# The parts of the maxima's rows on GpSimd instead of VectorE, with a changed pace of block A, sums one step later and a new hand-written order, in a kernel of two attention blocks

## The chip, the cores and the metric

The kernel runs on one core of one Trainium2 chip. The metric is the device time of one execution in microseconds (us). The time before is the median of three runs.

## The reference, cut to what matters

Two independent attention blocks over 2048 positions of width 640, 32 heads of 20, are computed and their outputs stand side by side. Block A looks at 8 positions (its own and every second one before it), block B at all 2048.

```python
def _A_ref(x, wqkv, wo):            # block A: a window of 8, dilation 2
    ...
    logits = jnp.einsum("bhsd,bhswd->bhsw", q, kg) * scale
    logits = jnp.where(mask[None, None, :, :], logits, -1e9)
    attn = _softmax(logits, axis=-1)
    o = jnp.einsum("bhsw,bhswd->bhsd", attn, vg)
    return (lambda x, *d: x.transpose(*d))(o, 0, 2, 1, 3).reshape(B, S, D) @ wo

def _B_ref(x, wqkv, wo):            # block B: full attention
    ...
    scores = jnp.einsum("bhqd,bhkd->bhqk", q, k) * (Dh ** -0.5)
    p = _softmax(scores, axis=-1)
    o = jnp.einsum("bhqk,bhkd->bhqd", p, v)
    return (lambda x, *d: x.transpose(*d))(o, 0, 2, 1, 3).reshape(B, S, D) @ wo

return jnp.concatenate([a, b], axis=-1)
```

## The kernel before, in words

**Stages.** First come the projections of A and of B and the rows of v of B. Then one long loop of 488 steps does nearly all of B's attention and, beside it, most of A's. Behind the loop stand 24 steps of B without maxima, and the output projection of B.

**Block B in the loop.** B is cut into 32 units (8 groups of 4 heads by 4 chunks of 512 queries), and a unit into 16 steps of 128 keys. One step needs, for each of the four heads, the following.

- A score matmul with keys on the partitions (`s_matmul`; output 128 x 512), and on ScalarE the exponential of it out of PSUM (`s_exp`, tile `e`).
- The matmuls of that `e` with v (`b_pv`, four accumulations side by side). After every second step ScalarE copies the sum to SBUF: the first of a unit to the tile `braw`, the seven others to a tile `more`, which GpSimd adds to `braw` (`pool(raws[u], raws[u], more)`). There are four `more` buffers, so that one comes round every eight steps.
- The maxima that a softmax needs. They are computed a second time from scores with queries on the partitions (`m_matmul`), 24 steps ahead (`LEAD`), and reduced out of PSUM by VectorE (tile `mx`).

When the maxima of a unit are complete, `max_rows` brings them into the two extra rows of the query tile `bq`, by which the score matmul subtracts them: VectorE reduces 64 values a partition to 16 and transposes 128 x 32 (`raw`), then splits that into a rounded part and the rest of it (tile `mtr`: one copy and one subtraction of 128 x 32). SP stores the parts to DRAM (`mdr`, four transfers), and loads them as rows of `bq` (two transfers). The steps of this are put off with `after(n, ...)`, which calls a function n steps later when the instructions are written out. A step is a place in the program, not a time.

**Order of the loop.** All engines run their instructions in the order in which the program writes them. A string `ORDER` writes the loop's order out by hand. `S` is two score halves, `Y` a score half and a maximum half, `M` and `N` two maximum halves with one reduction of 1024 columns or two of 512, `V` a step's `b_pv` (it also calls `begin`, which counts the step), `F` a piece of A's output projection and `j` a transpose of A. Digits name the PSUM banks. Eight banks serve all of it.

**Block A in the loop.** A goes in 16 tiles of 128 rows, each with eight units: four make scores (tile `akv` times `aq`, then halving sums into `al`), four weigh the values (`akv` times `al`, then sums into `ao`). All of that is GpSimd's. Between the two lies a softmax, of which VectorE does the maximum (`am`) and the reciprocal as "soft jobs". VectorE transposes the result (`turn`), DMAs carry it out and back, GpSimd splits it (`aot`) and `F` multiplies it with the output weights. Sixteen of the 128 units are done ahead of the loop.

**A's pace.** The class `InOrder` adds up an estimate of GpSimd's time, `gp.us`: for each tensor operation a constant and an amount per element. In each step from `A_FROM` on, `begin` writes out further instructions of A while the estimate is below step number x `STEP` (2.47 us) + `AHEAD` (2.4 us). All of GpSimd's tensor operations count in it, the sums of `braw` too.

**Names.** The profile gives every instruction one line, L66, the helper that writes them out; so its tiles tell them apart. Buffer numbers are left out (`mx4`, `mx1` are `mx`).

Of the kernel before, what the change touches and what calls it, by code (L numbers as in the profile page):

```python
# [10 lines left out]
F32 = mybir.dt.float32  # L11
# [37 lines left out]
A_FROM = 4  # L49


class InOrder:
# [6 lines left out]
    def __getattr__(self, name):  # L59
        op = getattr(self.engine, name)  # L60

        def emit(*a, **k):
            if name.startswith("tensor_"):
                n = math.prod(a[0].shape[1:])
                self.us += 0.25 + n * (0.00081 if name == "tensor_copy" else 0.00212)
            return self.tc.keep_in_program_order(op(*a, **k))  # L66
        return emit
# [3 lines left out]
def attention_pair(ctx, tc, xa, wqk_a, wv_a, wo_a, xb, wqk_b, wv_b, wo_b, oa, ob):  # L71
# [295 lines left out]
    def a_softmax(t):  # L367
# [8 lines left out]
        job(soft_jobs, 0, lambda: dve.tensor_reduce(m[:, 0], L.rearrange("p o h -> p h o"), AX.X, ALU.max))  # L376
# [11 lines left out]
        job(soft_jobs, 0, lambda: dve.reciprocal(m[:, 0], m[:, 0]))  # L388
# [217 lines left out]
    def max_rows(m4, m1, q, qc):  # L606
# [22 lines left out]
        after(t + 1, store)  # L629
        after(t + 2, load)  # L630
# [95 lines left out]
    def b_pv(i):  # L726
# [187 lines left out]
    def begin(i):  # L914
# [25 lines left out]
        "Y07M1S36M4V0Y71M4M2S06V7Y06M2S14Y75V0Y16M2S74VY71M5S42S03N17V4Y05S61M2VY07M5S13S42N70V1S36M4S72VY03M4S76V2Y30"  # L940
        "S17M4VjY03S16M4Y72V3S01jM4Y67VY02M4S61S73jY02jV6M4S71Y23VS70M4jS13Y26V7M4S01Y63VN05S41S23Y67M4S01N27V3S04M5Y21"
        "VY07M5S42S13N07V4S56M1Y03VY75S06M1Y34V7Y06S51M2VY06M4S13Y72V6Y03M4S17VY03M1S74Y56V3Y70M1S45VjY07S64Y51M2S07jV6"
        "jM4S13Y02VM4S73S02Y16jM4Y73jS06V2Y71M4S03VY07S16M4S32N70V1Y36M4S72VY07M2S64S51N70V6Y52M3S71VY70M1Y53S46V7M4S02"
        "Y61VN02S35M6S41S03N52V4Y07M5S31VY70M2S16S45N07V1Y26M3S05VY07M5Y24S31Y70V2Y13M5S74VY70M3S15Y26V7M0Y53S24VM0S26"
        "M4F3Y07M1S64Y35V0Y74S16M2VY71M4S63Y02V7S61M4Y03VY62S01M4Y37V6Y02S51M3VY70M1S53Y46V0Y75S13N24VN71S26M3S50S72N16"
        "V5Y70M3S21VY07M1S63S45N70V6Y14M2S75VY70M4S13jS26jV7jM0N53S42VN04S12Y56F7jjY05M1S36Y74V0Y35M1S76VY73M4S62Y01V7"
        "Y62M4S03VY06M1S35Y47V6Y03S52N14VN70S15M2N46F7Y05S41M2Y76V0S15M2Y74VS15M6Y23N04F1Y07S62M3Y51V0Y72S36M4VY71M2S64"
        "Y05Y17V6Y02M3S51VY70M1S53S46N07V5Y41M2S06VY70Y61M2S45Y07V6Y51S24Y03VM1S73Y45V0Y17M2S65VS71M5S42N30V7S61M4Y32V"
        "S06Y15N43N27F0Y16S52M3Y70V1Y26M3S75VY07M5S24S31N70V2S36M4Y71VY03S74M5Y12V0M3S75Y16VM3S75Y21V6S70N34Y51VY70M3"
        "S52Y16V7Y05S42N31VS06jS52jY34N17jF0jjY71S26M4Y03V7S62M4S01VM2S04Y56V1S07M2Y46VY07S25M3Y61V7Y02M3S56VY05M1S63"  # L950
        "S47N05V6S41M2Y70VY15S74M2Y06V1S75M2Y04VY75S06M2Y14V7Y06S53M1VY06M4S31S72N60V3Y74S56M1VY07M4S61S32N70V6Y51M3S72"
        "VY70M1S53S46N07V5Y41M2S06VY70Y61S42Y35S07N61V4Y35N62S01VM5Y70N13S24F7Y06M4Y12S73V0Y17M4S63VY71M2S64Y05V7Y64M2"
        "S01VY06M4Y13S72Y60V1Y72M4S36VY07M2S64S51N70V6Y52S73N41VY70S52M3Y16V7Y05M3S21VY02M5S14Y73V0Y14S25M6VjS14jM2M6"
        "Y50F1jjjY72M3S05Y61V7S02M3S65VM0S26Y34V5Y70M1S64VY07S63M1Y45V7Y60M1S34VS06M3S52N17V0S63Y45M1VY73M5S42S01N73V4"
        "Y05M6S12VY05M1S37S64N50V3Y27S16M4VY70M1S64S35N07V6Y41M2S05VY70M4S13S26N07V1Y25M3S06VY07M5S24S31N70V2S36M4Y71V"
        "Y03S74M5Y12F0Y71M5S42Y03V7Y42M5S01VY04M2S15Y76V0Y15M2S74VY71M5S42S30N17V4Y35S62M0VY73M5S20S14N37V2Y01M5S34VY70"
        "M3S15S26N07V1S25M3Y06VY72S03M4Y61V7S02jM4Y63VS02jS16jM4N37F0jjY71S26M4Y03V7Y62M4S01VY06M2S14Y75V0Y16M2S74VS71"
        "M5S42N30V7S61Y54M2VS04M5S17M2S04Y56V1Y07M2S46VY07S45M2S61N70V4Y35M6S21VY05M1S37S64N50V3Y27S16M4VY70M1S64S35N07"
        "V6Y41M2S05VY70M4S13S26N07V1Y25M3S06VY07M5S24Y31V0Y72M5S43VS71M3S25N60V7S14N32S65VM3Y06N21F5Y07M3S26Y51V0Y72S36"
        "M4VY71M2S64Y05V7Y64M2S01VY06M4S13Y27V6Y01M4S32VN70S13S24Y56N71V0Y26M3S75VY71M5S24Y03V1Y27M5S40VjY72M3M5S01jF7j"  # L960
        "jjY06S51M3Y72V0Y16M3S75VY71M5S24S03N17V2Y06S15M3VY07M5S14Y32V7Y01M5S43VS04M1S35N67V0S14Y32M5VS74M2S10M5S74Y32"
        "V1Y07M5S24VY07S23M5S41N70V2Y36M4S71VY07S16M4S32N70V1Y36M4S72VY07M2S64S51N70V6Y52M3S71VY70M1S53S46N07V5S41M2Y06"
        "VY74M2Y01S65V7Y06S24N35VY06M3M1S57F0Y73S46M1Y05V7S64M1S03VM5S04Y12V3Y07M5S42VY70S14M5Y23V0Y17M5S42VY71M3S25Y60"
        "V1Y72M3S56VY07M5S24S31N70V2Y36M4S71VY07Y16M4S32Y70V1S26M4Y73VY02M4M6S31jF0jjjY71M4S63Y02V7Y61M4S03VY06M1S35Y74"
        "V0Y35M1jS76VY73M4S62Y10V7Y62M4S31VS06M2S14Y57V0Y16M2S47VY14M5S72S30N41V7Y62M3S05VY06M1S53S74N06V5S73M1Y04VY73"
        "S06M1M4S73V0Y17M2S64S51M6VY52M3S17S06N25V1Y07M3S26VY07M5S24Y31V0Y72M5S43VS71M3S25N60V7Y14M2S65VY04S15M6S23N04"
        "V1S27N65Y03VY72S06M4N13F7Y02S14M5Y73V0Y14S25M6VY14M2S57S06N41V5Y07M2S46VS70Y16M2Y45V7Y60M2S14VY06M4S13Y72V6Y01"
        "M4S37VjS03jM1M4Y76F0jjjY71S26M4Y03V7Y62M4S01VY06M2S14S75N60V1Y72S36M4VY07M2S64S51N70V6Y52M3S71VY70M1S53S46N07"
        "V5S41M2S06VY74S03M1V6Y75S40M1VY75M3S02Y16V5Y70M3S21VY07M1S63S45N70V6Y14M2S75VY70M4S13S26N07V1Y25M3S06VY07M5S24"
        "S31N70V2Y36M4S71VY07Y16M4S32S70Y16V3Y27M4S06VN70S12M4S63Y71V0Y26S53N47VY16S25M3S70N61V2Y73S46N05VS71Y06M3N52F7"  # L970
        "Y06S15M3Y72V0M5S14Y73VM1S46Y75V3Y40S21M5VY70S42M5Y13V0Y74M5S21VjS74jM1M5Y30F7jjjY61M2S04Y75V6Y04M2S71VY70M4S13"
        "S26N07V1Y25M3S06VY07M5S24S31N70V2Y36M4S71VY07Y16M4S32Y70V1Y26S53N74VS02S73M5V4Y02S17M5VY03S12M5Y74V3Y01S25N67V"
# [12 lines left out]
        "Y03V7Y62M4S01VY06M2S14S75N60V1Y72S36M4VY07M2S64S51N70V6M2S75Y41VY70S52M3V1M6S05Y43VS07M5Y42V3Y70S16M4VY70S61j"
        "S25jM3N07F6jjjY70M3S52Y16V7Y05M3S21VY02M5S14Y73V0Y14M5S72VY71M3S25S06N17V2Y03S14M5VY70M3S15S26N07V1Y25M3S06V"
# [11 lines left out]
    for kind, *ns in re.findall("[A-Zj][0-7]*", ORDER):  # L998
# [90 lines left out]
```

## Time and profile before

| | us |
|---|---|
| median of three runs (1826.25 to 1831.67) | 1831.59 |
| the profiled execution's own time | 1828.4 |
| its span, first to last instruction | 1826.4 |
| busy in the span: TensorE, VectorE, ScalarE, GpSimd | 1779.4, 1387.3, 1328.9, 1197.8 |

In the profile PE is TensorE, PEld its weight loads, DVE VectorE, ACT ScalarE, POOL GpSimd and SP the queue that issues the DMAs. A group's row gives its count (x), its busy time, the mean of one in ns, and the engine's idle time just ahead of it with what ended that. The row of a window gives its length, and then busy time and count of each engine in the order PE, PEld, DVE, ACT, POOL, followed by the granted TensorE clock (1.00 is full), the DMA engines' share and GB/s; asked for one tile, it shows only the engines that work on that tile. A row of a timeline is start, duration, engine, operation, and in brackets the idle time ahead of it. The three score matmul groups of B are `ps_st<-bq,bk` (maxima), `ps_st<-bk,bq` (scores) and `ps_st<-e,vb` (values).

### The profile page before, as it was taken

Reading aid. Unit: us, or ns where it says so; the run is one execution under the profiler, and the core shown is the slowest. Engines: PE = TensorE matmul, PEld = TensorE weight load, DVE = VectorE, ACT = ScalarE, POOL = GpSimd, SP = SyncE. Lnnn points to the kernel's source line nnn. Section 1 sums busy time; section 2 is a strip of 40 time slices with the busy share of each in tenths; the row PEclk is TensorE's granted clock in tenths of the full one; section 3 lists DMA queues with packets and bytes.
Section 4 is the critical chain, followed back from the end, with each engine's and each line's share of the span. In section 5 each row is a group of like instructions: output and inputs, shape, how many; then the busy total and the mean of one; then the engine's idle time right before and its main releaser. Section 6 shows DMA issues by size and latency. Waiting matters only on the chain.

```text
span 1826.4 us, 31534 instructions
## 1 busy us (share of the span) xinstructions
PE 1779.4 (97%) x11211; PEld 997.6 (55%) x11211; DVE 1387.3 (76%) x1872; ACT 1328.9 (73%) x2593; POOL 1197.8 (66%) x1008
## 2 busy tenths in 40 slices
PE   9999999999999999999999999999999999999999
PEld 8988888887434444444444444444443443444469
DVE  3000333278999999999999999999999999999400
ACT  4222322223998899999899898989888888989981
POOL 0000079027899788898899898888888887635442
PEclk9999999999999999999999999999999999999999
DMA  6333687754642544353354425433533442212123
GB/s 229 114 97 114 199 300 259 245 171 135 178 131 82 135 131 124 112 163 112 114 138 114 138 89 160 139 116 90 162 116 104 120 129 92 48 51 80 50 69 111
DMA packets 191189, 240.21 MB, mean 132 GB/s; under 512 B 89020, under 2 KB 115260, under 8 KB 190040
## 3 DMA queue, kind: packets, MB, share of 16 engines
q1 hardware_dynamic: 190456, 237.54, 43.4%
q8 instruction: 88, 1.44, 0.3%
q14 instruction: 69, 0.57, 0.1%
q10 hardware_dynamic: 576, 0.66, 0.1%
HBM read 173.21 MB, written 64.91 MB: 130 GB/s over the span
## 4 chain that ended last, share of the span: by engine, by line
PE 69%; DVE 23%; DMA 2%; POOL 2%; issue 2%; ACT 2%; SPq 0%; DVEq 0%; POOLq 0%; ACTq 0%
PE ps_st L66 69%; DVE mx L66 20%; DVE mtr L66 3%; DMA bk<-kb_d 2%; ACT e L66 1%; POOL akv L66 1%; POOL braw L66 0%; DMA s_d<-braw 0%; DMA akv<-va_d 0%; DVE turn L66 0%; DMA akv<-ka_d 0%; DVE am L66 0%; ACT more L66 0%; POOL aot L66 0%; DMA bq<-qb_d 0%
## 5 line engine op out<-in xcount | busy, mean ns | idle before, releaser
L66 DVE TENSOR_REDUCE mx<-ps_st 128x1 f32<-128x512 f32 (+1 forms) x1486 | 1214.5, 884 | 50.1 <-PE ps_st L66 47.1
L66 ACT ACTIVATE e<-ps_st 128x512 f32<-128x512 f32 x2048 | 1065.4, 614 | 68.8 <-PE ps_st L66 49.4
L66 PE MATMUL ps_st<-bq,bk 62*128 62x512 f32 x2048 | 559.6, 441 | 23.1 <-DVE mx L66 21.7
L66 PE MATMUL ps_st<-bk,bq 60*128 60x512 f32 x2048 | 543.6, 444 | 16.5 <-DVE mx L66 14.4
L66 PE MATMUL ps_st<-e,vb 128*32 128x512 f32 x4096 | 548.1, 610 | 1.2 <-ACT e L66 0.3
L66 PEld LDWEIGHTS ps_st<-bq,bk 62*128 62x128 f32 x2048 | 279.5, 185 | 467.2 <-ACT e L66 280.4
L66 POOL TENSOR_TENSOR braw<-braw,more 128x512 f32<-128x512 f32 x224 | 288.3, 1287 | 191.0 <-ACT more L66 187.9
L66 POOL TENSOR_TENSOR akv<-akv,aq 128x1280 f32<-128x1280 f32 x64 | 188.5, 2945 | 234.6 <-DMA akv<-ka_d 234.6
L66 PEld LDWEIGHTS ps_st<-bk,bq 60*128 60x128 f32 x2048 | 248.5, 185 | 117.4 <-DVE mx L66 70.6
L66 POOL TENSOR_TENSOR akv<-akv 128x640 f32<-128x640 f32 (+3 forms) x304 | 283.7, 933 | 14.2
L66 ACT COPY ro<-ps_st 128x320 f32<-128x320 f32 (+2 forms) x124 | 61.4, 497 | 221.9 <-PE ps_st L66 172.5
L66 PEld LDWEIGHTS ps_st<-e,vb 128*32 128x32 f32 x4096 | 82.2, 108 | 154.9 <-issue 75.0
L66 POOL TENSOR_TENSOR akv<-akv,al 128x1280 f32<-128x1280 f32 x64 | 152.1, 2376 | 0.2
L66 ACT COPY more<-ps_st 128x512 f32<-128x512 f32 x224 | 133.8, 597 | 11.8 <-PE ps_st L66 9.3
L66 PE MATMUL ps_st<-wc,xn 128*128 128x512 f32 (+1 forms) x576 | 133.4, 376 | 0.0
L66 PE MATMUL ps_st<-ww,xn 128*128 128x320 f32 x768 | 127.6, 317 | 0.0
L66 PEld LDWEIGHTS ps_st<-ww,xn 128*128 128x128 f32 x768 | 114.9, 190 | 20.1 <-ACT e L66 7.9
L66 PEld LDWEIGHTS ps_st<-wc,xn 128*128 128x128 f32 x576 | 106.4, 188 | 17.6 <-ACT xn L66 0.2
L66 PE MATMUL ps_st<-xn,w 128*128 128x512 f32 x480 | 115.8, 390 | 0.0
L66 PEld LDWEIGHTS ps_st<-xn,w 128*128 128x128 f32 x480 | 90.1, 188 | 19.4
L66 ACT CAST pr<-ps_st 128x512 fp32r<-128x512 f32 x40 | 23.6, 589 | 101.0 <-PE ps_st L66 101.0
L66 DVE TENSOR_TENSOR pr<-ps_st,pr 128x512 fp32r<-128x512 f32 x40 | 27.7, 692 | 90.6 <-ACT pr L66 87.8
(64 smaller groups left out, 1027.3 us busy)
## 6 DMA issues: line engine op xcount, KB each, us to landing
akv<-ka_d SPq DMA_DIRECT2D x128, 320.0 KB
akv<-va_d SPq DMA_DIRECT2D x128, 320.0 KB
kb_d<-pr SPq DMA_DIRECT2D x20, 512.0 KB
qb_d<-pr SPq DMA_DIRECT2D x20, 512.0 KB
bk<-kb_d SPq DMA_DIRECT2D x16, 640.0 KB
bq<-qb_d SPq DMA_DIRECT2D x64, 160.0 KB
rb<-s_d SPq DMA_DIRECT2D x128, 64.0 KB
stg<-xb SPq DMA_DIRECT2D x12, 512.0 KB
```

Of the source, the lines that this page charges most:

```text
L66: return self.tc.keep_in_program_order(op(*a, **k))
```

## The change

1. The copy and the subtraction behind the transpose of a unit's maxima move from VectorE to GpSimd (`parts`). The store of them is written out one step later, and the load too.
2. A soft job of A's softmax may be written out by `begin` three steps after it is given; before, it was written out at the start of A's next unit.
3. The estimate of GpSimd's time has a constant of 0.2 us instead of 0.25, and 0.0017 us instead of 0.00212 an element for the operations with four dimensions (the weighing of the values). A starts at step 1 instead of 4.
4. The sum of `braw` and `more` is written out two steps after the copy instead of one.
5. A piece of A's output that isn't ready at its `F` is kept (`owed`) and tried again at each later step; before, its bank stayed in the list of given banks.
6. `ORDER` is new. In both strings a unit's maxima are complete 7 to 10 steps ahead of its first score matmul, and there are 488 `V` and 32 `F`.

| in `ORDER` | S | Y | M | N | reductions (M + Y + 2N) | steps from one pair of F to the next | step of the last F |
|---|---|---|---|---|---|---|---|
| before | 661 | 630 | 514 | 147 | 1438 | 30.9 on average | 466 |
| after | 647 | 658 | 517 | 130 | 1435 | 28.5 on average | 434 |

```diff
-A_FROM = 4
+A_FROM = 1
...
-                self.us += 0.25 + n * (0.00081 if name == "tensor_copy" else 0.00212)
+                self.us += 0.2 + n * (0.00081 if name == "tensor_copy" else 0.0017 if len(a[0].shape) == 4 else 0.00212)
...
-        job(soft_jobs, 0, lambda: dve.tensor_reduce(m[:, 0], L.rearrange("p o h -> p h o"), AX.X, ALU.max))
+        job(soft_jobs, 3, lambda: dve.tensor_reduce(m[:, 0], L.rearrange("p o h -> p h o"), AX.X, ALU.max))
...
-        job(soft_jobs, 0, lambda: dve.reciprocal(m[:, 0], m[:, 0]))
+        job(soft_jobs, 3, lambda: dve.reciprocal(m[:, 0], m[:, 0]))
...
             dve.transpose(raw, m1)
-            dve.tensor_copy(mt[:, 1], raw)
-            dve.tensor_tensor(mt[:, 2], raw, mt[:, 1].bitcast(F32), ALU.subtract)
+
+        def parts():
+            gp.tensor_copy(mt[:, 1], raw)
+            gp.tensor_tensor(mt[:, 2], raw, mt[:, 1].bitcast(F32), ALU.subtract)
...
         after(t, turn)
-        after(t + 1, store)
-        after(t + 2, load)
+        after(t, parts)
+        after(t + 2, store)
+        after(t + 3, load)
...
-            after(1, pool, raws[u], raws[u], more, ALU.add)
+            after(2, pool, raws[u], raws[u], more, ALU.add)
...
+        if soft_jobs and soft_jobs[0][0] <= now[0]:
+            run_jobs(soft_jobs, 1)
...
     ORDER = (
-        "Y07M1S36M4V0Y71M4M2S06V7Y06M2S14Y75V0Y16M2S74VY71M5S42S03N17V4Y05S61M2VY07M5S13S42N70V1S36M4S72VY03M4S76V2Y30"
...
+        "Y07M1M3Y56V0Y71M3N25Y06V7Y04M2S15Y76V0Y15M2S74VY71M5S42S03Y17V4Y05S76M2VN05S71S62M3S07N51V6Y02S53N74VS05M1S73"
...
+    owed = []
+
+    def out_owed():
+
+        while owed:
+            given.append(owed[0])
+            if not out_piece():
+                given.clear()
+                break
+            owed.pop(0)
+
...
+        elif kind == "F":
+            owed += ns
+            out_owed()
         else:
-            given += ns
-            if kind == "F":
-                out_piece()
-                continue
             if not left_a[0] and not WO_b:
                 load_out(wo_b, WO_b)
             begin(i)
+            out_owed()
+            given += ns
```

More of the change, by code (lines that the diff above doesn't have):

```diff
@@ L944, in attention_pair @@
[L944 to L948, printed above, removed]
@@ L994, in attention_pair @@
[L994 to L996 removed]
+        "Y07M1M3Y56V0Y71M3N25Y06V7Y04M2S15Y76V0Y15M2S74VY71M5S42S03Y17V4Y05S76M2VN05S71S62M3S07N51V6Y02S53N74VS05M1S73"
+        "Y46V0M1S75Y36VjM1S74Y56V3jY70M1S46VjY07S64Y51M2S70V6jM4S31jY72VM4S03S17Y26Y05M3Y61V7Y02M3S65VY06M1S53Y74V0Y35"
@@ new lines, in attention_pair @@
+        "Y06S51Y23N74V0S13M5Y72VS13N74Y56N20F1Y72S36M4Y01V7Y62M4S03VY06M1S35S74N60V3Y72S16M4VY70M1S64S35N07V6Y41S02Y53V"
+        "M0S72Y34V5Y06S71N42VY07M3S61Y25V7Y60S14N32VY06S15M3Y27V6Y01M3S52VS70M1M3M5F7Y04S31Y25N76V0Y15N43S72VY71S26Y54"
+        "N03V7S64M1Y05VS64S03jN21jY57jF6jjY70M1S35Y46V7Y05M1S34VY03M5S41S72N30V4Y57S36M1VY07M5S31S42N70V3Y41M5S72VY70M1"
+        "S46Y35V0Y74S16M2VY71M4S63Y20V7Y61M4S32VY06M2S14S75N60V1Y72S36M4VS07M2S64N51V0S72Y36M4VS76M2S10M4S76Y32V1Y07M4"
+        "S26VY07S23M4S61N70V2Y36S75Y14VM6S05Y43V1Y02S76N53VY07S24M5S31N70V2Y36M4S71VY07Y16M4M2Y70F1Y72S36M4Y01V7Y62M4"
@@ new lines, in attention_pair @@
+        "Y36M4S01VY07Y16M4S32Y70V1Y26M4S73VY07M2S64S51N70V6Y52M3S71VY70M1S53S46N07V5Y41M2S06VY70Y61M2S45S07V6M4Y31S02V"
+        "S75M3S02N16V7Y05S41M2VY06M4Y13S72Y60V1S72M4Y36VY07M4M2S61F0Y71M2Y46S05V7Y04M2S15VY06M4S13Y72Y60V1Y75M3S26VY07"
+        "M5S24Y31V0jS72jM5S43jVjM1S74Y56V3jY70M1S46VY07M4S61M2Y70F6Y70S15M2Y46V7Y05S13Y24VM0S63Y45V2Y01M6S35VY01M3S75"
+        "Y62V0Y17M3S56VY75M1Y63S04V5Y67M1S04VY07M3S62S15N70V6Y14M2S75VY70M4S13S26N07V1Y25M3S06VY07M5S24S31N70V2Y36M4S71"
+        "VY07S16N35S42N70V1S36M4Y72VS03M4M6Y21F0Y72S36M4Y01V7Y62M4S03VY06M1S35S74N60V3S72M5S41VY07M5S42V1Y07S34M5VY07"
@@ new lines, in attention_pair @@
+        "Y02V1Y76M4S30VY72S06M4Y31V2Y07M4S63VY07S16M4S32N70V1Y36M4S72VY07Y62M4S31N70S62V3S41M5S72VM0S74Y56V2Y73M0S64V"
+        "Y73M5S04Y12V3Y07M5S41VY70M1S46S53N07V4S56M1Y03VY75S06M1M3F7Y06M1S35Y74V0Y35M1S76VY73M4S62Y01V7Y62M4S03VY06M1"
+        "S35Y47V6S03jM1Y54VS70jS15jM2N46F7jjY06M2S14Y75V0Y16M2S74VY71M5S42S03N17V4Y05S61M2VY07M5S13Y42V7Y03S61M4VY06M2"
+        "S14Y57V0Y16M2S45VY71M4S63S02N17V6Y05S41M2VS70M4S13N26V7S05Y41M2VS01M4S67M2S01Y45V6Y70M2S51VY70S54M2S16N07V5Y41"
+        "M2S06VM0S74M2S56V7S01M4Y63VY02S16M4Y37V0Y16S25M3VY71M5S24Y03Y17V2Y06M4S31VY07Y16M4M2Y70F1Y72S36M4Y01V7Y62M4S03"
@@ new lines, in attention_pair @@
+        "Y15M6VY02M4S17S63N02V1S74M5Y03VS72jM5S04Y31jV7jY06M1S54VjM5S03S42N17jS06S53N14V2Y01M6S54VY03S15Y74N62V3Y40S15"
+        "M6VY04M1S57S63N40V5Y67S41N23VY07S64M1N35F0Y71S26M3Y05V7Y61M3S02VY06M1S53Y74V0Y35M1S76VY73M4S62Y10V3Y76M4S21V"
+        "Y07M1S64Y53V7Y60M1S45VY06M4M1Y37F6Y05M1S73Y46V0Y75M1S34VY73M5S42Y01V7Y24M5S03VS04M1Y35Y67V0Y14N32S56VY71M4S63"
+        "N02F7Y06S51M3Y72V0S16M3Y75VY61Y72S34N50V6S71M2Y54VS70N15S23N64V7S05M1Y63VY04M1S56Y73F0Y71S26M4Y03V7Y62M4S01V"
+        "Y06M2S14S75N60V1Y72S36M4VY07M2S64Y51Y70V6Y52S13Y74VM1S03Y45V7Y60S12N35VY06S14M2S57N60V1Y25M3S76VY07M5S24Y31V0"
@@ new lines, in attention_pair @@
+        "Y72M5S43VY71M3S25S60N17V2Y36M4S01VY07S16M4Y32Y70V1Y63M4S27VY06M2S74S15N60V7Y14M2S65VY06M4Y13S72Y60V1Y72M4S36V"
+        "Y07M2S64S51N07V6Y52S34M0VY75M2S40S16N75V4S03M1Y76VS05M1S73Y64V0M1S75Y34VM1S75M3S60Y71Y25V6Y70S14M2VY70M4S13S26"
+        "N07V1Y25M3S06VY07M5S24S31N70V2Y36M4S71VY07S16M4S32N70V1Y36M4S72VY07M2S64S51N70V6Y52M3S71VY70M1S53Y46Y70V5S41M2"
+        "Y67VS04M2S16N75V0S14M2Y76VS15M2S74Y60V1N72S35Y40VY72S36M4S01N27V3Y04M5S21VY70M1S46S53N07V4Y56M1S03VY07M5S31S42"
+        "N70V3Y41M5S72VY70M1S46S35N07V4Y36M1S05VY07M5S31S42N70V3Y41M5S72VY70M1S46Y35V0M6S14M2VS71M5S40M2S71M5")
```

81 lines of the change are left out of this document (30 added, 51 removed).

## The prediction, made before the result was known

> **What bounds the kernel now.** I read the page first: the shares of the engines, the 40 slices, the chain of work that ended last.
>
> ```profile
> PE 1779.4 (97%) x11211; PEld 997.6 (55%) x11211; DVE 1387.3 (76%) x1872; ACT 1328.9 (73%) x2593; POOL 1197.8 (66%) x1008
> ...
> DVE  3000333278999999999999999999999999999400
> ...
> PE 69%; DVE 23%; DMA 2%; POOL 2%; issue 2%; ACT 2%; SPq 0%; DVEq 0%; POOLq 0%; ACTq 0%
> ```
>
> VectorE's 76% is a mean over stages: nearly nothing at both ends, and 9 in every slice of the loop. So the change, which works in the loop, has to be read from the loop. Its first steps are written from 446 us on, and its last reduction ends near 1712. The windows, all instructions first, then those of the tile `e` alone:
>
> ```profile
> 446.00:1712.00 1266.00, 1226.94 (x8288) 540.65 (x8287) 1238.25 (x1697) 1140.01 (x2243) 1041.48 (x861) 0.99 0.41 116
> 600.00:1100.00 500.00, 490.02 (x3336) 219.18 (x3334) 493.29 (x682) 455.54 (x898) 439.67 (x368) 1.00 0.44 125
> 900.00:1000.00 100.00, 99.69 (x689) 44.86 (x686) 98.95 (x139) 93.11 (x185) 89.74 (x79) 1.00 0.44 120
> ```
>
> ```profile
> 600.00:1100.00 500.00, 207.80 (x1560) 30.74 (x1560) 405.39 (x780) 1.00 0.44 125
> ```
>
> The loop is 1266 us for 488 steps, 2.594 a step (four exponentials are a step: 780 / 4 = 195 in the 500 us). In it VectorE is busy 1238.25 / 1266 = 97.8%, TensorE 96.9%, ScalarE 90%, GpSimd 82%. Two engines are nearly full, so I ask what VectorE does there. The groups of VectorE, shapes apart, window 446 to 1712:
>
> ```profile
> L66 DVE TENSOR_REDUCE mx<-ps_st 128x2 f32<-128x1024 f32 x512 | 620.3, 1216 | 3.5 <-PE ps_st L66 2.6
> L66 DVE TENSOR_REDUCE mx<-ps_st 128x1 f32<-128x512 f32 x923 | 595.9, 681 | 20.6 <-PE ps_st L66 18.4
> L66 DVE TENSOR_TENSOR mtr<-mtr 128x32 fp32r<-128x32 f32 x30 | 25.1, 837 | 1.0
> L66 DVE CAST mtr<-mtr 128x32 fp32r<-128x32 f32 x31 | 22.8, 735 | 1.1
> ```
>
> The last two are the instructions that the change takes away. 837 and 735 ns for 32 elements a partition are odd beside 681 for 512. The tile `mtr` by itself gives the spread, and the timelines of the two engines around one unit's end the reason:
>
> ```profile
> L66 DVE CAST mtr<-mtr x32: 181/828/1973, 416.8 to 1711.9; 128x32 fp32r<-128x32 f32 x32
> L66 DVE TENSOR_TENSOR mtr<-mtr x32: 191/812/2295, 417.9 to 1712.1; 128x32 fp32r<-128x32 f32 x32
> ```
>
> ```profile
> 634.03 1.03 DVE L66 CAST mtr<-mtr 128x32 fp32r<-128x32 f32 x1
> 635.09 1.20 DVE L66 TENSOR_TENSOR mtr<-mtr 128x32 fp32r<-128x32 f32 x1
> ```
>
> ```profile
> 633.45 1.57 POOL L66 TENSOR_TENSOR akv<-akv 128x640 f32<-128x640 f32 x1
> 634.96 1.28 POOL L66 TENSOR_TENSOR braw<-braw,more 128x512 f32<-128x512 f32 x1
> ```
>
> The copy ends at 635.06, GpSimd's running sum at 635.02; the subtraction ends at 636.29, GpSimd's next sum at 636.24. VectorE waits inside its instruction for GpSimd's to end; alone it needs 181 and 191 ns. No reduction may pass meanwhile, and TensorE finds no free bank. The worst unit end shows it on TensorE:
>
> ```profile
> 1287.60 1.07 PE L66 MATMUL ps_st<-e,vb 128*32 128x512 f32 x8
> ...
> 1291.92 0.49 PE L66 MATMUL ps_st<-bq,bk 62*128 62x512 f32 x1 [2.58 <-DVE mx L66]
> ...
> 1292.57 1.93 PE L66 MATMUL ps_st<-e,vb 128*32 128x512 f32 x8
> ```
>
> TensorE idles 2.58 us, and the next values group takes 1.93 instead of 1.07 (the granted clock of 1280 to 1300 is 0.91, in a row below).
>
> **The change part by part.** *Parts off VectorE.* 22.8 + 25.1 us, and 0.8 for one subtraction that the trace lacks: **48.7 us** leave an engine that is 97.8% full. What VectorE keeps is 1189.6 us; reductions fall from 1438 to 1435, worth nothing. At the same share of the loop that is 1189.6 / 0.978 = 1216 us, **50 less**. TensorE is late next: its 1226.94 us at the best share shown (99.69 of 100, 900 to 1000) make 1231 us, **35 less**. Its busy time need not be all work, as ends are modelled, so I take the middle, 1224 us, **42 less**. If the idle time behind VectorE's stalls goes too and it reaches the 98.95% of 900 to 1000, it is 1202, 64 less: the lower end.
>
> *Parts on GpSimd.* The nearest rows, for the window 446 to 1600:
>
> ```profile
> L66 POOL TENSOR_TENSOR am<-am 128x32 f32<-128x32 f32 x14 | 3.5, 253 | 1.1
> L66 POOL CAST ww<-stg 128x320 fp32r<-128x320 f32 x2 | 0.9, 452 | 3.1 <-DMA stg<-wo_a 3.1
> L66 POOL CAST aot<-back 128x640 fp32r<-128x640 f32 x15 | 10.8, 721 | 0.6 <-PE ps_st L66 0.6
> ```
>
> The subtraction has its own size there, 0.253 us. Casts of 320 and 640 differ by 0.269, so 32 elements need about 0.21 (bounds 0.18, what VectorE needs unhindered, and 0.452). 31 x 0.46 = 14 us, 0.029 a step, beside other work as long as GpSimd has room. A rule speaks against the move: the Trainium skill, GPSIMD Engine Reference, section 4.1 Engine selection, keeps elementwise work on VectorE since GpSimd takes about twice as long with two inputs. By that the pair would cost 0.37 x 2 = 0.74 us and 23 us of GpSimd, an estimate; the trace's own pair for the subtraction, 0.191 and 0.253, lies nearer together. The sum on VectorE stays as it is.
>
> *The later store and load.* The maxima are complete 7 to 10 steps ahead of their use. The reduction stands one or two steps behind, the load now 4 or 5: at least 3 steps, some 7.5 us, are left. SP's timeline has the need:
>
> ```profile
> 636.32 1.74 SPq L66 DMA_DIRECT2D mdr<-mtr  x4
> 639.11 0.54 SPq L66 DMA_DIRECT2D bq<-mdr  x2
> ```
>
> 2.8 us from store to load. The parts now queue behind a running GpSimd instruction, for which VectorE stood at most 2.3 us. Nothing is charged; if GpSimd ran over 5 us late, TensorE would wait for `bq`, and behind SP's waiting store stand A's loads.
>
> *A's pace.* By the diff's formula a tile (42 instructions) counts 55.5 us before and 51.2 after; sums and parts take 0.67 of the 2.47 a step. That is 55.5 / 1.80 = 30.8 steps a tile before, 28.5 after; the 14 tiles left for the loop need some 400 steps instead of 431. What GpSimd really needs: 439.67 us for 195 steps is 2.255 a step, of it 8 x 1.288 / 16 = 0.644 for `braw`; A's 1.611 x 30.8 / 28.5 = 1.741, and with `braw` and parts 2.41 a step. Adding up the means of a tile's groups I get 2.48. At 2.51 a step (1224 / 488) GpSimd is 96 to 99% full: no charge, no reserve.
>
> *Sums two steps later, soft jobs three.* What GpSimd waited for between 446 and 1600:
>
> ```profile
> POOL braw L66 <- ACT more L66: 95.5, 49, 5.8
> POOL al L66 <- DVE am L66: 32.5, 20, 3.9
> ```
>
> A step more is 2.5 us, about the mean of the 49 waits (1.9), so most of the 95.5 should go. The `more` buffers come round after eight steps, which leaves six. The soft jobs cost VectorE one wait of 1.7 us; between nothing and 3 us are won there, and I count 0. `owed` costs nothing if the pieces are ready, and their distance in the string (28.5 steps) fits A's pace.
>
> **The sum.** 1828.4 - 42 = 1786 by the profiled execution, whose median of runs lies 3 higher: **1788 us**.
>
> **Rivals.** *GpSimd becomes the bound (slower).* It needs 2.48 us a step without waits, over some 400 steps; waits that its slack hid come on top. Those quoted were 95.5 + 32.5 = 128 us in the 444 steps to 1600, 0.29 a step. No gain is left at 2.594 - 2.48 = 0.114 a step, 40% of them. If 60% stay (0.17), 400 x 2.65 + 88 steps x 2.49 (VectorE's 1216 / 488) = 1279 us, 13 more than now: **1841**. If 25% stay (0.07), it is 400 x 2.55 + 219 = 1239, or 1801. For it: 96 to 99% full, and a new wait of GpSimd for VectorE's transpose at each unit. Against: a queue that runs late finds its data ready, so its waits shrink by themselves.
>
> *TensorE is the bound.* Then only its waits for VectorE go. Its 96.9% and the 69% of the chain speak for it:
>
> ```profile
> L66 PE MATMUL ps_st<-bq,bk 62*128 62x512 f32 x1957 | 544.1, 442 | 23.1 <-DVE mx L66 21.7 <-ACT e L66 1.1
> L66 PE MATMUL ps_st<-bk,bq 60*128 60x512 f32 x1947 | 523.6, 443 | 13.5 <-DVE mx L66 12.7 <-ACT e L66 0.2
> ```
>
> 21.7 + 12.7 = 34 us: **1794**, still inside the forecast. The Trainium skill (Trainium Kernel Development and Optimization, section Performance Expectations) calls matmul busy time a bad metric and trusts weight-load time: 540.65 of 1266 is 43%, which by that page is no bound, and VectorE's 1216 us alone would stand, 1778; the trace so far sides with it in that TensorE, 97% busy, still loses time to VectorE's stalls.
>
> *The stalls are covered, and nothing moves.* Then the pace would be the same with and without them. Exponentials in windows of 20 us, of 62 such from 460 to 1700 (last count), and `mtr` in the third of these windows:
>
> ```profile
> 460.00:480.00 20.00, 9.98 (x76) 1.58 (x80) 17.91 (x37) 1.00 0.66 161
> 1260.00:1280.00 20.00, 7.34 (x63) 1.10 (x56) 16.40 (x33) 1.00 0.47 132
> 1280.00:1300.00 20.00, 8.89 (x64) 1.15 (x56) 13.67 (x26) 0.91 0.62 157
> 1680.00:1700.00 20.00, 9.47 (x72) 1.29 (x69) 16.93 (x34) 1.00 0.27 87
> ```
>
> ```profile
> 1280.00:1300.00 20.00, 3.39 (x3) 0.91 0.62 157
> ```
>
> The 40 windows with under 0.95 us of `mtr` have 32.8 on average, the 12 with over 1.9 have 28.4. So stalls do cost, and this rival (1828) is weak.
>
> *The new order packs worse.* It has no row. The nearest is the pace that the old order had in its last stage, 1600 to 1712, without A's load and with 2.6 us of `mtr`:
>
> ```profile
> 1600.00:1712.00 112.00, 44.75 (x336) 6.61 (x336) 89.79 (x174) 1.00 0.21 62
> ```
>
> 174 / 4 = 43.5 steps, 2.575 each; at that pace throughout the loop takes 1257 us: **1819**.
>
> **How the numbers follow.** The forecast, with TensorE's case in it and GpSimd's light one, 1768 to 1806: 0.62. Part of the gain lost to GpSimd's waits or the order, 1806 to 1826: 0.15, like 1819 above. Nothing moves, 1826 to 1837: 0.07. Slower, GpSimd the bound at around 1841: 0.16. About 0.3%, 5.5 us, is what a measurement of this kernel can tell from no change; so faster 0.77, same 0.07, slower 0.16. The range runs from VectorE's best (1764, drawn in to 1768) to 1832, past the order's case and into the case of no change. Between 0.15 and 0.2 lie outside, nearly all above.
>
> **What would show it.** Right: no `mtr` in VectorE's groups; GpSimd casts 128x32 in about 0.21 us and subtracts in 0.25; 195 steps in some 490 us instead of 500; TensorE's waits for `mx` below the 34 us, and no 20 us window of the loop at a clock of 0.91; GpSimd above 95% until A's last `akv` near 446 + 405 x 2.51 = 1463 us (now 1577), its waits for `more` below 40; last reduction near 1670. Wrong: ScalarE's copies to `more` waiting for `braw`, TensorE waiting for `bq<-mdr`, or SP's store waiting for GpSimd by several us (GpSimd is the bound); reductions as dense as now with ScalarE's or TensorE's waits grown by the 48.7 us (another bound, or the order).

## The result, and the profile after

The changed kernel takes **1777.89 us** (median of 4 runs, 1776.97 to 1780.57), against 1828.92 for the kernel before beside it (1822.69 to 1831.67). The ratio is 0.9728, with a 95% interval of 0.9698 to 0.9759: 51 us, or 2.7%, faster. The profiled execution took 1777.45 us.

A correction to the names given above: `ps_st<-bq,bk`, with 62 rows, is the score matmul (`bq` carries the two extra rows of the maxima), and `ps_st<-bk,bq`, with 60, the matmul for the maxima. No sum used which is which.

First the page of the changed kernel: the shares of all engines, VectorE's and GpSimd's slices, and the chain.

```profile
PE 1760.9 (99%) x11211; PEld 996.6 (56%) x11211; DVE 1337.9 (75%) x1805; ACT 1323.5 (75%) x2593; POOL 1209.8 (68%) x1072
...
DVE  3100232268999999999999999999999999999300
...
POOL 0000059227899999999999999899999962445241
...
PE 77%; POOL 13%; DVE 3%; issue 2%; DMA 2%; ACT 2%; SPq 1%; POOLq 0%; ACTq 0%; DVEq 0%
```

VectorE's share of the chain fell from 23% to 3%, though its slices in the loop still show 9. GpSimd's rose from 2% to 13%; the kernel with the parts alone, below, is as fast with 2%. Now the windows of the loop (first step written out to last reduction, 443 to 1658 here, 446 to 1712 before), the same 500 us as before, and A's part of the loop.

```profile
443.00:1658.00 1215.00, 1208.28 (x8283) 541.39 (x8283) 1189.72 (x1632) 1134.95 (x2244) 1049.30 (x920) 1.00 0.43 121
600.00:1100.00 500.00, 498.95 (x3434) 225.01 (x3434) 490.80 (x675) 468.31 (x928) 484.31 (x423) 1.00 0.49 139
443.00:1440.00 997.00, 992.21 (x6815) 447.52 (x6817) 976.17 (x1345) 929.40 (x1840) 958.55 (x833) 1.00 0.48 137
```

The loop is 1215 us instead of 1266, and those 51 us are the whole gain. TensorE's columns say where they come from. Its idle time in the loop fell from 1266 - 1226.94 = 39.1 us to 1215 - 1208.28 = 6.7, which is 32.3. Its busy time fell from 1226.94 to 1208.28 for practically the same matmuls (8288 and 8283 records), which is 18.7. So some of what stood as busy before was no work. Part of it is the clock, whose mean rose over the span:

```profile
core 0: 1826.4 us, clock 0.992
```

```profile
core 0: 1775.6 us, clock 0.998
```

The first row is the kernel before, the second the one after. 0.006 of 1826 us is 11 us (an estimate from these two rows).

The tile `mtr` of the changed kernel shows the moved instructions at work:

```profile
L66 POOL CAST mtr<-mtr x32: 201/212/258, 416.8 to 1658.4; 128x32 fp32r<-128x32 f32 x32
L66 POOL TENSOR_TENSOR mtr<-mtr x32: 252/253/262, 417.1 to 1658.7; 128x32 fp32r<-128x32 f32 x32
```

On VectorE the same pair took 181 to 2295 ns, on GpSimd it takes 201 to 262. The groups of TensorE in the loop (443 to 1658) give the waits:

```profile
L66 PE MATMUL ps_st<-bq,bk 62*128 62x512 f32 x1954 | 544.8, 440 | 2.9 <-DMA bq<-mdr 1.6 <-DVE mx L66 1.0 <-ACT braw L66 0.2
L66 PE MATMUL ps_st<-bk,bq 60*128 60x512 f32 x1946 | 520.1, 439 | 1.6 <-DVE mx L66 1.4
```

Of the 34.4 us that both waited for `mx`, 2.4 are left.

### The profile page after: what moved, and what is told of

Read it like the earlier page. It is cut to its first block, busy times and chain, and to the rows that moved or that the text cites. A ratio compares the mean times of both kernels' runs of the same rounds, so it can differ in the third digit from the quotient of the medians.

```text
span 1775.6 us, 31540 instructions
## 1 busy us (share of the span) xinstructions
PE 1760.9 (99%) x11211; PEld 996.6 (56%) x11211; DVE 1337.9 (75%) x1805; ACT 1323.5 (75%) x2593; POOL 1209.8 (68%) x1072
## 4 chain that ended last, share of the span: by engine, by line
PE 77%; POOL 13%; DVE 3%; issue 2%; DMA 2%; ACT 2%; SPq 1%; POOLq 0%; ACTq 0%; DVEq 0%
PE ps_st L66 77%; POOL akv L66 7%; DVE mx L66 3%; POOL braw L66 3%; POOL ao L66 1%; ACT e L66 1%; SPq L66 1%; DMA bq<-qb_d 1%; POOL al L66 1%; DMA stg<-wv_b 0%; POOL aot L66 0%; DMA stg<-xa 0%; ACT more L66 0%; DMA ot_b<-braw 0%; DMA rb<-s_d 0%
```

## The experiments

Two theories stood at the start. **Theory 1**: the parts alone make the gain, because VectorE's instruction stood still until a running GpSimd instruction ended, and TensorE found no free bank meanwhile. **Theory 2**: the new order, A's pace and the later sums make a good part of it. Later the question became what bounds the loop now, and why a stalled VectorE costs what it costs. The expectations number their theories each for itself. In every set the kernel before had a median between 1828 and 1830 us.

### The parts alone

The kernel before, with this and nothing else of the change; the two instructions don't count in A's pace:

```diff
             dve.transpose(raw, m1)
-            dve.tensor_copy(mt[:, 1], raw)
-            dve.tensor_tensor(mt[:, 2], raw, mt[:, 1].bitcast(F32), ALU.subtract)
+        def parts():
+            us = gp.us
+            gp.tensor_copy(mt[:, 1], raw)
+            gp.tensor_tensor(mt[:, 2], raw, mt[:, 1].bitcast(F32), ALU.subtract)
+            gp.us = us
...
-        after(t + 1, store)
-        after(t + 2, load)
+        after(t, parts)
+        after(t + 2, store)
+        after(t + 3, load)
```

> The kernel before with one part of the change: copy and subtraction on GpSimd, store and load one step later; old order, old pace of A (the two instructions are left out of the estimate of GpSimd's time, so that the program is otherwise the same). Theory 1 (VectorE stood still behind GpSimd's instructions, and that alone was the price): 35 to 50 us faster than before, that is 1779 to 1794. Rival 2 (the new order and pace bring the gain): within 6 us of before, 1823 to 1834. Rival 3 (both share it): around 1805.

Measured: 1775.76 us (1774.62 to 1777.55), ratio 0.9713 (0.9679 to 0.9748). That is the whole gain of the change. Its windows:

```profile
443.00:1660.00 1217.00, 1208.14 (x8294) 537.42 (x8296) 1192.53 (x1636) 1135.50 (x2243) 1052.49 (x923) 1.00 0.43 121
600.00:1100.00 500.00, 498.77 (x3426) 221.27 (x3424) 492.28 (x676) 469.14 (x927) 455.96 (x397) 1.00 0.47 132
```

TensorE and VectorE stand as in the changed kernel. Only GpSimd is less full (456 of 500 us instead of 484): A ends later, its last `akv` at 1525.5 instead of 1436.2, and that changes nothing about the end.

The two traces also say where the time was lost. This program differs from the kernel before in nothing but the pair with its store and load, so their steps can be laid side by side, each from its first exponential to that of the next. Added up over the units of the loop, the kernel before takes 49.7 us longer: 0.3 us in the steps 0 to 7 of a unit's 16, 50.7 in the steps 8 to 13, and 1.4 less in the last two. All but one of the reductions that end a unit's maxima, with the pair right behind them, start in the steps 7 to 11. So the loss stands behind the pair and nowhere else.

### The rest of the change alone

The changed kernel with the parts on VectorE again:

```diff
             dve.transpose(raw, m1)
-
-        def parts():
-            gp.tensor_copy(mt[:, 1], raw)
-            gp.tensor_tensor(mt[:, 2], raw, mt[:, 1].bitcast(F32), ALU.subtract)
+            dve.tensor_copy(mt[:, 1], raw)
+            dve.tensor_tensor(mt[:, 2], raw, mt[:, 1].bitcast(F32), ALU.subtract)
...
-        after(t, parts)
```

> The changed kernel with copy and subtraction back on VectorE, all else as changed. Theory 1: the gain is lost, 1822 to 1835, and since GpSimd is busier (96 to 99%) the two instructions take as long or longer than before, 0.75 to 1.1 us each. Rival 2: stays within 8 us of the changed kernel, 1775 to 1786. Rival 3: around 1800 to 1810.

Measured: 1849.79 us (1848.23 to 1857.76), ratio 1.0126 (1.0085 to 1.0168). It is 72 us behind the changed kernel and 22 behind the kernel before, worse than expected. Its tile `mtr`:

```profile
L66 DVE CAST mtr<-mtr x32: 181/742/2698, 416.8 to 1739.7; 128x32 fp32r<-128x32 f32 x32
L66 DVE TENSOR_TENSOR mtr<-mtr x32: 191/1196/2873, 418.0 to 1739.9; 128x32 fp32r<-128x32 f32 x32
```

and TensorE's wait in its loop, up to 1730:

```profile
PE ps_st L66 <- DVE mx L66: 47.0, 43, 3.7
```

Of all 64 instructions of the pair 17 take under 0.25 us here, 22 in the kernel before; together they need 59.9 us instead of 49.5, and TensorE waits 47.0 us for `mx` instead of 34.4. The profiled execution is the slowest of the four, 1857.8 us, 29 over that of the kernel before. The waits are 13 of these, and the clock, 0.985 over the span instead of 0.992, about 13 more (an estimate). Laid beside the changed kernel step by step, 74 of 79 us are lost in the steps 8 to 12 of the units, so this loss too stands behind the pair. Why the pair is caught more often (GpSimd is hardly fuller: 444.58 of 500 us from 600 on, 439.67 before), no run isolates. Without the move, the rest of the change is a loss.

### The old order, and the sums one step later

First the changed kernel with the whole of the old string:

```diff
     ORDER = (
-        "Y07M1M3Y56V0Y71M3N25Y06V7Y04M2S15Y76V0Y15M2S74VY71M5S42S03Y17V4Y05S76M2VN05S71S62M3S07N51V6Y02S53N74VS05M1S73"
+        "Y07M1S36M4V0Y71M4M2S06V7Y06M2S14Y75V0Y16M2S74VY71M5S42S03N17V4Y05S61M2VY07M5S13S42N70V1S36M4S72VY03M4S76V2Y30"
...
```

> The changed kernel with the old hand-written order, all else as changed. Theory 1: 1778 to 1792, since the order matters little. Rival 2: 1810 to 1830. Rival 3: around 1800.

Measured: 1787.18 us (1783.42 to 1789.17), ratio 0.9773 (0.9736 to 0.9809). With A's new pace the old order costs 9 us; with A's old pace (the parts alone, above) it costs nothing. So order and pace seem to belong together (the new order with the old pace was not run), and together they bring nothing over the old pair.

Then the changed kernel with its sums written out one step after the copy, as before:

```diff
-            after(2, pool, raws[u], raws[u], more, ALU.add)
+            after(1, pool, raws[u], raws[u], more, ALU.add)
```

> The changed kernel with the sums written out one step after the copy instead of two. If GpSimd has no reserve at 96 to 99% (the rival of the prediction), its waits for the copies come back, some 50 to 100 us of them, and the time rises by 10 us or more, above 1788. If GpSimd off the critical path takes them up, the time stays within 4 us of the changed kernel, 1775 to 1782.

Measured: 1776.55 us (1775.79 to 1782.73), ratio 0.9726 (0.9681 to 0.9771). The later sums are worth nothing that can be measured.

### The parts on VectorE by another instruction

Theory 1 has two readings. The form of VectorE's instruction may make it wait for GpSimd, or any work at that place would cost as much. Here the changed kernel gets the copy and the subtraction back on VectorE, as reductions.

```diff
-            gp.tensor_copy(mt[:, 1], raw)
-            gp.tensor_tensor(mt[:, 2], raw, mt[:, 1].bitcast(F32), ALU.subtract)
+            dve.tensor_reduce(mt[:, 1], raw.unsqueeze(2), AX.X, ALU.max)
+            dve.tensor_reduce(mt[:, 2], mt[:, :2].bitcast(F32).rearrange("p t c -> p c t"), AX.X, ALU.subtract)
```

> The changed kernel with the parts back on VectorE, but as two reductions (the copy as a maximum over one element, the rest as a difference reduced over two), in place of a copy and a subtraction of two tiles. Theory 1a: it is the form of the instruction that waits for GpSimd, since the reduction of 64 values just ahead never took over 0.221 us in any trace; then both take 0.2 to 0.25 us whatever GpSimd does, and the time is 1778 to 1795 (up to 31 x 0.45 = 14 us of VectorE more than the changed kernel). Rival 1b: what waits is anything of VectorE's at this place, between the transpose and SP's store, whatever its form; then they take 0.75 to 1.1 us each and the time is 1835 to 1858 as with the parts back on VectorE.

Measured: 1790.5 us (1788.62 to 1793.06), ratio 0.9788 (0.9757 to 0.9818). The tile `mtr`:

```profile
L66 DVE TENSOR_REDUCE mtr<-mtr x64: 185/204/227, 415.4 to 1674.1; 128x32 fp32r<-128x32 f32 x32, 128x32 fp32r<-128x64 f32 x32
```

Same engine, same place, same data, the same busy GpSimd, and no instruction takes more than 227 ns, where a copy took up to 2698. So the form decides. The Trainium skill, SBUF — State Buffer, section Who interferes with whom, says why this may be: VectorE shares one pair of ports with GpSimd; a copy in its two-port mode takes that pair, and whoever comes second is blocked for the whole instruction; an operation with two inputs in SBUF contends with GpSimd's reads; and a reduction never contends. The 227 ns beside the 2698 agree. That the ports are the reason no run here shows. The unhindered pair still takes 31 x 0.41 = 12.6 us of VectorE, and the kernel is 12.6 us slower than the changed one. That the two agree says little: the same work can cost less than itself or nothing, as the added transposes below show.

### No work of A in the loop

The changed kernel twice, first with the parts on VectorE as a copy and a subtraction, then on GpSimd. Both leave out block A's attention behind its first sixteen units, and with it A's output:

```diff
-A_FROM = 1
+A_FROM = 10 ** 6
...
-            if not left_a[0] and not WO_b:
+            if i == 440:
```

> Parts on VectorE as a copy and a subtraction, and all of block A's attention behind its first units and its output left out, so that GpSimd has little but the sums (some 25% of the loop). Not to be compared in time, only the two instructions' durations. Theory 1 (they wait for a running GpSimd instruction): at least two thirds of the 32 copies and subtractions take 0.18 to 0.2 us, the rest up to 1.3 us, the length of a sum; together below 20 us in place of 58. Rival: they are long for another reason, and stay at 0.8 us or above in the median.

Measured, parts on VectorE, one execution: 1829.53 us. Half right. The medians fall to 182 and 193 ns, but the two still take 35.7 us together, not under 20, and 38 of 64 are short, where two thirds were expected. The sums into `braw` that are left on GpSimd still catch the pair. Rows of its timeline around one unit's end:

```profile
629.72 1.31 POOL L66 TENSOR_TENSOR braw<-braw,more 128x512 f32<-128x512 f32 x1 [2.92 <-ACT more L66]
629.93 1.16 DVE L66 TENSOR_TENSOR mtr<-mtr 128x32 fp32r<-128x32 f32 x1
...
633.40 0.79 PE L66 MATMUL ps_st<-bk,bq 60*128 60x512 f32 x1 [2.29 <-DVE mx L66]
...
635.68 1.93 PE L66 MATMUL ps_st<-e,vb 128*32 128x512 f32 x8
```

The subtraction starts behind the sum and ends 0.06 us after it (631.09 and 631.03). All 26 that take over 0.25 us in this run start while a GpSimd instruction runs and end 0.03 to 0.06 us after it, and so do all 47 with the rest of the change alone and all 42 in the kernel before.

> As the run without block A's attention behind its first units and without its output, but with the parts on GpSimd as in the changed kernel (the same part of the computation is left out). VectorE's two instructions took 35 us there. If VectorE's own time is the price: 25 to 40 us less than that run's 1829, 1790 to 1805. Theory 2 (a stall costs more than itself, by TensorE's idling and lower clock): 50 us less or more, below 1780, with no 20 us window of the loop at a granted clock under 0.95. If A's absence makes the loop slow for another reason: 1820 to 1830.

Measured, parts on GpSimd: 1792.54 us (1784.54 to 1792.95), ratio 0.979 (0.9761 to 0.982). That is 37 us below the other, for VectorE's 35.7, though the other is a single execution and these four spread over 8 us: again about one to one, and not the 50 or more that Theory 2 gave. What I had not expected is that it is 15 us *slower* than the changed kernel, which does A's work too. Its windows and waits:

```profile
443.00:1674.00 1231.00, 1183.53 (x7842) 485.22 (x7842) 1171.82 (x1529) 1123.03 (x2200) 360.79 (x344) 0.97 0.18 46
600.00:1100.00 500.00, 478.83 (x3190) 195.03 (x3182) 476.52 (x620) 457.52 (x897) 132.08 (x124) 0.97 0.18 45
```

```profile
PE ps_st L66 <- DVE mx L66: 31.1, 31, 2.4
PE ps_st L66 <- ACT e L66: 14.2, 19, 1.5
```

441 matmuls are gone, yet TensorE waits 45 us, at a mean clock of 0.97. Of 60 windows of 20 us, 20 have a clock of 0.83 to 0.96, in the changed kernel only the last. My reading: `F`'s matmuls filled places in the order at which the banks of B aren't free yet; without them TensorE idles there, and the idling costs clock. That reading is argued from the trace; no run isolates it.

### What bounds the loop now

Work added to the changed kernel tells it. First 122 transposes of 128 x 32 on VectorE, one every fourth step:

```diff
+    scr = sb.tile([128, 32], F32, tag="scr", bufs=1, name="scr")
...
+        if loop[1] and i % 4 == 0:
+            dve.transpose(scr, ident[:, :32])
```

> The changed kernel with one needless transpose of 128x32 on VectorE in every fourth step (122 x 0.21 to 0.24 = 26 to 29 us of VectorE). If VectorE sets the loop's pace now: 20 to 29 us more, 1798 to 1807. If TensorE does (the prediction's engine that is late next): under 8 us more, below 1786. If both stand at the limit by turns: 10 to 20 more.

Measured: 1777.16 us (1775.58 to 1779.14), ratio 0.9711 (0.9676 to 0.9746). 24.2 us more on VectorE cost nothing. Its loop:

```profile
443.00:1658.00 1215.00, 1209.52 (x8279) 534.91 (x8278) 1192.95 (x1749) 1133.35 (x2239) 1046.67 (x919) 1.00 0.43 121
```

VectorE's busy time rose by only 3.2 us. The records explain it: they overlap. A 128x512 reduction is shown with 0.68 us, and the next starts 0.598 us after it (median of 916 starts in the changed kernel; 1.131 for 1024 columns). A wait of up to 0.08 us therefore counts as busy. Summed from start to start, each form at its near-shortest (the 8th percentile), VectorE needs 1169 of the 1215 us. So 46 us are waits, of which the 97.9% shows 25, and a transpose, about 0.12 us from start to start, goes into them.

Then one score matmul written twice, every fourth step:

```diff
         pe.matmul(p, k[rows, pl, kb * 128:kb * 128 + 128], q[rows, qc, pl], start=True, stop=True)
+        if loop[1] and i % 4 == 0 and pl == 0 and r == 0:
+            pe.matmul(p, k[rows, pl, kb * 128:kb * 128 + 128], q[rows, qc, pl], start=True, stop=True)
```

> The changed kernel with one score matmul done twice in every fourth step (122 x 0.2 to 0.3 = 24 to 37 us of TensorE). If TensorE sets the pace now: 20 us more or above, 1798 up. If VectorE does: under 8 us more, below 1786. If both by turns: 10 to 20 more.

Measured: 1790.34 us (1789.2 to 1790.92), ratio 0.9785 (0.9756 to 0.9815). Its loop:

```profile
443.00:1671.00 1228.00, 1222.68 (x8400) 553.09 (x8400) 1195.37 (x1632) 1136.06 (x2243) 1048.11 (x920) 1.00 0.42 120
```

12.5 us for 122 matmuls, 0.10 each; TensorE's busy time rose by 14.4 and its idle time stayed small (5.3 us). That is in the bracket that I had given to two engines by turns. With the nothing of the transposes beside it, I take TensorE for the pace of the changed loop, and my price of a matmul for too high. That is argued from these two runs, not isolated.

The same transposes in runs of two, every eighth step:

```diff
-        if loop[1] and i % 4 == 0:
-            dve.transpose(scr, ident[:, :32])
+        if loop[1] and i % 8 == 0:
+            for _ in range(2):
+                dve.transpose(scr, ident[:, :32])
```

> The same 122 transposes two in a row in every eighth step. Theory 2: between the spread ones (no cost) and four in a row, 1778 to 1790. Rival: within 4 us of the changed kernel.

Measured: 1788.93 us (1787.92 to 1789.45), ratio 0.978 (0.9754 to 0.9806).

And in runs of four, every sixteenth:

```diff
-        if loop[1] and i % 4 == 0:
-            dve.transpose(scr, ident[:, :32])
+        if loop[1] and i % 16 == 0:
+            for _ in range(4):
+                dve.transpose(scr, ident[:, :32])
```

> The changed kernel with the same needless transposes of VectorE as in the run that spread them (122 in all, 24 us), but four in a row in every sixteenth step. Theory 2 (what costs is how long VectorE frees no bank at a stretch, since TensorE then runs out of banks, idles and loses clock; spread work costs nothing): 10 to 25 us more than the changed kernel, 1788 to 1803. Rival (only VectorE's total counts, and it has reserve): within 4 us of the changed kernel, 1774 to 1782, as when spread.

Measured: 1797.04 us (1794.94 to 1798.83), ratio 0.9825 (0.9802 to 0.9848). The same work (122, 122 and 124 transposes) costs 0, 11 and 19 us, as VectorE frees no bank for about 0.2, 0.45 and 0.94 us at a stretch. One such stretch, and TensorE's groups in the loop of that kernel:

```profile
728.97 0.94 DVE L66 STREAM_TRANSPOSE scr<-ident 128x32 f32<-128x32 f32 x4
```

```profile
L66 PE MATMUL ps_st<-bq,bk 62*128 62x512 f32 x1952 | 552.2, 441 | 9.4 <-DVE mx L66 8.7
L66 PE MATMUL ps_st<-bk,bq 60*128 60x512 f32 x1946 | 523.6, 440 | 4.0 <-DVE mx L66 3.7
```

Its wait for `mx` is 12.4 us instead of 2.4, about half of the 19. The rest stands in TensorE's busy records (1219.1 us instead of 1208.3), and with the runs of two nearly all does (1220.2). The clock stayed at 1.00 in both, so the lost clock of Theory 2 has no part in it. At the changed kernel's prices from start to start, VectorE needs 1182 to 1186 us in the three.

The place in a unit could be the reason instead of the length: the runs of four all stand at a unit's first step. Laid beside the changed kernel step by step, they lost 20.4 us in the two steps behind it, the runs of two 6.4 us there and 5.3 in the two steps behind a unit's ninth, the single ones 0.5 behind the first. At the same place, the length of a stretch decides, not the sum. The copy and subtraction together were such a stretch, 1.6 us on average and up to 3.2 in the kernel before. As two reductions they were a shorter one: from the reduction that ends a unit's maxima to the next of `ps_st`, VectorE takes 0.89 us there, 0.41 in the changed kernel and 2.07 in the kernel before.

### How near GpSimd is

The changed kernel with two memsets of 128 x 32 more on GpSimd in every step:

```diff
+    scr = sb.tile([128, 32], F32, tag="scr", bufs=1, name="scr")
...
+        if loop[1]:
+            for _ in range(2):
+                gp.memset(scr, 0.0)
```

> The changed kernel with two needless memsets of 128x32 on GpSimd in each step (2 x 488 x 0.13 = 130 us, outside the estimate that paces A). GpSimd idles 38 us in 443 to 1440, and 400 steps of this add 107. If GpSimd becomes the bound there, as the prediction's slower rival has it: 40 to 70 us more than the changed kernel, 1818 to 1848. If lateness of GpSimd is covered by the buffers and the slack of the maxima: under 8 us more.

Measured: 1857.86 us (1857.82 to 1859.49), ratio 1.016 (1.0137 to 1.0183). The memsets, 976 x 0.125 = 122 us in all, cost 80 us, more than expected. Window, and the waits of its loop:

```profile
443.00:1440.00 997.00, 951.09 (x6357) 422.53 (x6356) 913.01 (x1254) 868.87 (x1714) 953.15 (x1510) 0.98 0.45 129
```

```profile
PE ps_st L66 <- DMA bq<-mdr: 30.2, 9, 6.7
PEld ps_st L66 <- DMA bq<-mdr: 12.3, 4, 5.9
DVE am L66 <- POOL al L66: 22.1, 7, 11.2
```

By these waits GpSimd sets the pace here: the parts come late, the rows of `bq` come late, and a soft job stands on VectorE up to 11.2 us for GpSimd. In the changed kernel GpSimd idles 997 - 958.55 = 38 us up to 1440, so the distance to this is short.

## Why the prediction was right, point by point

**What VectorE loses: right.** What it keeps was to be 1189.6 us and is 1189.72, the loop 1216 at the same share and is 1215. That sum alone gave 1778. The kernels with the parts alone and with all but the parts show that this term is the whole gain. One reading in it was wrong: the subtraction "that the trace lacks" is there, at 1712.1 us, just behind the window, and takes 0.19 us instead of 0.8. That moves nothing.

**TensorE is late next: mis-sized.** The step that was off is "at the best share shown ... make 1231 us, 35 less", which pulled the forecast from 50 to 42 us. The share was nearly reached (99.4%), but of 1208.28 us and not of 1226.94. The 18.7 us between them, waiting and slow clock inside the records, were no work. About 10 of them are the clock (0.99 and 1.00 in the rows of the loop; 11 us over the span, above); the rest is not split further. I had named that possibility and gave it half; it deserved all. The rival that only TensorE's waits go, 1794, failed for the same reason: the waits for `mx` fell by 32 as it said, and the busy time by 18.7 on top. The Trainium skill's rule beside it (Trainium Kernel Development and Optimization, section Performance Expectations: matmul busy time is a bad metric for how close a kernel is to its roofline, weight-load time a good one) came out right on matmul busy time in the kernel before. The page speaks of the distance from the roofline; the prediction used it to tell what bounds the loop, and for that it doesn't carry to the kernel after: weight loads are 541.39 of 1215 us there, 45%, and still TensorE seems to set the pace.

**VectorE as the bound: right in size, wrong in kind.** The sum treated its 97.8% as full. The added transposes show that single short instructions cost nothing, the runs of them that long stretches do. 48.7 us of instructions bought 51, by my reading, because they stood in stretches of 1.6 us, not because VectorE had no room. What TensorE lost by them was 32 us of waits, some 10 of clock and some 9 more inside its records. The term of 50 us had none of these in it, so its size is in part luck: other work of VectorE cost anything from nothing (the single transposes) to its own time (the two reductions).

**Parts on GpSimd: right.** 0.21 and 0.25 us were expected, 0.212 and 0.253 came, and nothing was paid. The rule of the Trainium skill against it (GPSIMD Engine Reference, section 4.1 Engine selection) gives its factor of two for two inputs alone and calls one input roughly line-rate. So the 0.74 us of the prediction, which doubled the copy too, was more than the rule says; by it the pair would take 0.181 + 2 x 0.191 = 0.56 us, an estimate, and 0.465 came. The engine that is slower alone was the faster one here, since VectorE's 181 and 191 ns came only where no GpSimd instruction was under way, or one that was just beginning or in its last 0.2 us.

**The later store and load: almost right.** Nothing was charged; once TensorE waited 1.55 us for it. Timeline of the changed kernel:

```profile
556.65 0.54 SPq L66 DMA_DIRECT2D bq<-mdr  x2
...
558.34 0.18 PEld L66 LDWEIGHTS ps_st<-bq,bk 62*128 62x128 f32 x1 [1.84 <-DVE mx L66]
558.37 0.47 PE L66 MATMUL ps_st<-bq,bk 62*128 62x512 f32 x1 [1.55 <-DMA bq<-mdr]
```

**A's pace: right, and worth nothing.** A's last `akv` starts at 1436 (1463 expected), GpSimd is 97% full in 600 to 1100, and its waits up to 1440 are small:

```profile
POOL mtr L66 <- DVE mtr L66: 7.4, 4, 3.8
POOL ww L66 <- DMA stg<-wo_a: 3.2, 3, 1.2
POOL al L66 <- DVE am L66: 2.5, 2, 2.0
```

None for `more` is among them, where 95.5 us stood, and the 32.5 for `am` are 2.5. The prediction put this down to the later sums, and that was the wrong reason: with the sums as early as before, the waits for `more` are 1.8 us up to 1440. They shrank by themselves, as it argued against its rival. And nothing of it reached the time: going back to earlier sums changed nothing, nor did A's later end with the parts alone.

**The rivals.** GpSimd as the bound: a real mechanism, not reached; two memsets a step bring it about. Stalls that cost nothing: excluded by the parts alone. An order that packs worse: the new one doesn't with the new pace, where the old one is 9 us slower.

**The signs to look for** came as named: no `mtr` copy on VectorE; exponentials in 600 to 1100 up from 780 to 806, so 195 steps in 484 us (490 expected); one 20 us window of the loop below full clock, the last, at 0.92; last reduction at 1656.5 (1670 expected).

## What to carry to other kernels

A short instruction that takes several times its shortest duration is waiting for something: lay the other engines' timelines beside it and see whose instruction ends when it ends. Then there are two remedies, another engine or another form of the instruction; here the first was worth 51 us and the second 39. A busy share of 97% settles neither that an engine is the bound nor that it isn't: add a little work to it, once spread and once in a run, and see what that costs.

## What the runs showed of the hardware

**The clock falls after shorter idling than I thought.** One idle stretch of 2.58 us (kernel before, in the prediction's rows) or 2.29 us (no work of A) was followed by values groups of 1.93 us instead of 1.07; so was a pair of 0.97 and 0.86 us (no work of A, parts on GpSimd):

```profile
862.21 0.49 PE L66 MATMUL ps_st<-bq,bk 62*128 62x512 f32 x1 [0.97 <-ACT e L66]
863.56 0.79 PE L66 MATMUL ps_st<-bk,bq 60*128 60x512 f32 x1 [0.86 <-DVE mx L66]
...
865.56 1.93 PE L66 MATMUL ps_st<-e,vb 128*32 128x512 f32 x8
```

The granted clock in windows of these two runs, the first two rows from the one with 2.29 us (idle up to 633.40), the third from the one with the pair:

```profile
630.00:632.00 2.00, 0.62 (x3) 0.18 (x1) 2.00 (x2) 1.17 (x3) 1.04 (x1) 1.00 0.01 1
632.00:639.00 7.00, 5.59 (x21) 2.35 (x21) 5.56 (x8) 2.17 (x4) 0.00 (x0) 0.51 0.07 16
```

```profile
863.00:870.00 7.00, 6.44 (x29) 2.39 (x29) 4.53 (x7) 3.66 (x8) 0.00 (x0) 0.51 0.00 0
```

In both it fell to about a half before the idling was over.

A single 1.55 us (changed kernel, above) was not followed by such groups: the next took 1.06 at a clock of 1.00. The Trainium skill, TensorE: Matmul & The Clock Gate, Part 1, names a window of about 3.4 us for this, running freely; the stretches here are shorter than that window, and the measurement decides.

**Less work can be slower.** Without A's part of the loop the same kernel took 1792.5 us instead of 1777.9, at a clock of 0.97 instead of 1.00 in the loop. Why is argued above, not isolated.
